# Two of four operand sums made by accumulating transfers in a Fourier-mixing kernel

## The chip, the core and the metric

The kernel runs on one core of a Trainium2 chip. The metric is the device time of one execution in microseconds. One execution of each kernel is recorded by the hardware profiler; its lines are shown below as "profile".

A core has TensorE (PE, matrix products, with its weight loads shown as PEld), VectorE (DVE), ScalarE (ACT), GpSimd (POOL) and SyncE (SP). In this kernel SP issues all transfers, in the order of its own instruction stream, and an instruction that waits holds back what stands behind it on its engine.

## The reference, cut to what matters

```python
xn = layernorm(x)                                  # x: 2048 x 512, float32
a = xn @ dft_hid_re.T ; b = xn @ dft_hid_im.T      # 512 x 512
s = dft_seq_re @ a - dft_seq_im @ b                # 2048 x 2048
h = relu(xn @ w1 + b1) ** 2                        # hidden size 1792
g = silu(h @ w2 + b2)
out = x + s * g
```

## The kernel before

The kernel reorders the Fourier part: it first multiplies the normalised x with the sequence matrices (called C, the cosines and sines, 2048 x 2048 each) and then with the hidden matrices (`wd`). Every product is made in three passes of reduced-precision float32: an operand is split into a high half and a low half (`split`: ScalarE writes the high half, VectorE subtracts it from the source to get the low one), and the passes are high x high, high x low and low x high.

The columns of C are cut into eight blocks of 256 (`c`), the rows of C in steps (`j`, eight for each block). Blocks 0 and 1 (`PLAIN = 2`) are done with plain products, while x is being loaded and normalised. Blocks 2 to 7, the C stage, use Winograd's form of Strassen's scheme: one step takes the four sub-blocks I11, I12, I21, I22 of C (each 128 partitions x 256 columns, I22 etc. being places in the raw tile `r`) and needs, beside three of them as they are, four sums T1 to T4. The seven products of the step accumulate in seven banks M[1] to M[7] over the eight steps of a block; at the block's end VectorE and ScalarE combine the banks into four results and split them for `stage2`, which multiplies with `wd` (lines 493 to 509).

For one step the preparation is `load_c` (a transfer of 512 KB into `r`, three buffers) and `moving` (line 167): the sums into `t` (two buffers), then the split of `r` into `g0` (three sub-blocks, 768 columns) and the split of `t` into `g1` (four sums, 1024 columns); `g0` and `g1` have two buffers each. The sums are made by VectorE, in `winograd_moving`:

```python
t[:, 0:2] = r[I12] - r[I11:I22+1]     # L162, one instruction of 512 columns
t[:, 2]   = r[I22] - t[:, 0]          # L164, 256 columns
t[:, 3]   = t[:, 2] - r[I21]          # L165, 256 columns
```

Two steps are prepared ahead of their products (`AHEAD = 2`, `prep` at line 465). In the C stage there is other work beside the steps: `stage2` of the block before at steps 2 and 3, and jobs that prepare the weights of the second part (`make_w1`, `make_w2`) and store them in DRAM. After the C stage come the hidden products (`hidden`, line 404) and the outer products (`outer`, line 439).

The order of the instructions on each engine is not the order of the source: the program is built with a scheduler that plays the program through with its own costs and places each instruction on its engine's stream when it would be ready (`schedule_with_timeline_sim=True`, line 573). The order is then fixed; a change of one instruction can move others.

The names in the lines of the profile: `m` are the banks M, `g` the split operands `g0` and `g1`, `r` the raw tile, `t` the tile of sums, `xc` the stationary operand, `yps` the banks of `stage2`, `pq` its operands, `w1raw` a raw tile of w1, `hps` and `ops` the hidden and outer products.

Of the kernel before, what the change touches and what calls it, by code (L numbers as in the profile page):

```python
# [10 lines left out]
ALU = mybir.AluOpType  # L11

P = 128
# [3 lines left out]
CW = 256  # L17
# [5 lines left out]
PLAIN = 2  # L23
# [6 lines left out]
I12, I11, I22, I21 = range(4)  # L30
# [13 lines left out]
def fnet_gated_kernel(ctx, tc, x, xt, ct, wd, w1, w2, b1, b2, out):  # L44
    nc = tc.nc
# [5 lines left out]
    def split(hi, lo, src):  # L51
        cut[0] = nc.scalar.activation(hi, src, AF.Copy)  # L52
        return nc.vector.tensor_tensor(lo, src, hi.bitcast(F32), op=ALU.subtract)  # L53
# [14 lines left out]
    def bank(name):  # L68
        return acc.tile([P, 512], F32, tag="bank", name=name)

    def t2k(name):
        return pool.tile([P, 512], F32, tag="t2k", bufs=4, name=name)

    def buf(tag, shape, name, dtype=F32, bufs=1):
        return pool.tile(shape, dtype, tag=tag, bufs=bufs, name=name)
# [53 lines left out]
    def sums(g):  # L129


        s = xn32[ND * g, "tile"].rearrange("p j h (b n) -> p j (h b) n", b=2)
        t = s1[g] = buf("t", [P, ND, CW], f"s1_{g}", bufs=2)
        nc.vector.tensor_tensor(t, s[:, :, 1], s[:, :, 3], op=ALU.add)
        nc.vector.tensor_tensor(s[:, :, 1], s[:, :, 1], s[:, :, 0], op=ALU.subtract)
        nc.vector.tensor_tensor(s[:, :, 0], t, s[:, :, 0], op=ALU.subtract)
        return nc.vector.tensor_tensor(s[:, :, 2], s[:, :, 2], s[:, :, 0], op=ALU.subtract)

    def split_sums(j):
# [6 lines left out]
    raw, part = {}, {}  # L146

    def load_c(c, j, hs=slice(0, 2)):
        if (c, j) not in raw:
            raw[c, j] = buf("r", [P, 4, CW], f"r{c}_{j}", bufs=3)  # L150
        q = slice(2 * hs.start, 2 * hs.stop)
        nc.sync.dma_start(raw[c, j][:, q], ct[c, j, :, q])

# [7 lines left out]
    def winograd_moving(t, r):  # L161
        nc.vector.tensor_tensor(t[:, 0:2], r[:, I12:I12 + 1].to_broadcast([P, 2, CW]), r[:, I11:I22 + 1],  # L162
                                op=ALU.subtract)
        nc.vector.tensor_tensor(t[:, 2], r[:, I22], t[:, 0], op=ALU.subtract)  # L164
        nc.vector.tensor_tensor(t[:, 3], t[:, 2], r[:, I21], op=ALU.subtract)  # L165

    def moving(key, r):

        g0 = buf("g0", [P, 2, 3, CW], f"g0_{key}", F32R, bufs=2)
        g1 = buf("g1", [P, 2, 4, CW], f"g1_{key}", F32R, bufs=2)  # L170
        t = buf("t", [P, 4, CW], f"t_{key}", bufs=2)
        winograd_moving(t, r)
        split(g0[:, HI], g0[:, LO], r[:, I11:I21 + 1])
        split(g1[:, HI], g1[:, LO], t)
        return g0, g1
# [17 lines left out]
    def pq(c, m, dh, src=None):  # L193
        t = PQ[c, m, dh] = buf(f"pq{m}{dh}", [P, 2, 512], f"pq{c}_{m}_{dh}", F32R)
        if src is not None:
            split(t[:, HI], t[:, LO], src)
        return t

    def stage2(c, t):
        ps = bank(f"yps{c}_{t}")  # L200
        n = 0
        for m in range(2):
            for k in range(ND):
                w = (k % 2) * CW + t * P
                for a_, b_ in PASSES:
                    nc.tensor.matmul(ps, PQ[c, m, k // 2][:, a_, w:w + P], WD[m, k][:, b_, :],  # L206
                                     start=n == 0, stop=n == 2 * ND * 3 - 1)
                    n += 1
        if t == 0:
            ysb[c] = buf("sx", [P, 2, D], f"ysb{c}")  # L210
        y = ysb[c][:, t]
        nc.scalar.activation(y, ps, AF.Copy)
        nc.sync.dma_start(Y[2 * c + t], y)

    def mm(ps, w, mv, first, last):

        for d in range(2):
            for a_, b_ in PASSES:
                nc.tensor.matmul(ps[:, d * CW:(d + 1) * CW], w[:, a_, d * P:(d + 1) * P], mv(b_),  # L219
                                 start=first and d == 0 and (a_, b_) == (HI, HI),  # L220
                                 stop=last and (a_, b_) == (LO, HI), skip_group_check=True)
# [10 lines left out]
    def xt_half(c, q):  # L232


        st = xt_stage(c, q)
        if q == 0:
            flat = rows.rearrange("a b -> (a b)")
            xT["rows"] = st[0]
            for m in range(2):
                for h in range(2):  # L240
                    n = m * S + c * TC + h * 256
                    nc.sync.dma_start(st[0][:, 2 * m + 1 - h], bcast(flat[n:n + 256], 256))
        r, t = st[-2:]
        mr = xT["rows"]
        nc.sync.dma_start(r, xt[c, q])
        for k in range(2):
            nc.vector.tensor_tensor(r[:, 2 * k:2 * k + 2], r[:, 2 * k:2 * k + 2], mr[:, 0:2], op=ALU.subtract)
            nc.vector.tensor_tensor(r[:, 2 * k:2 * k + 2], r[:, 2 * k:2 * k + 2], mr[:, 2:4], op=ALU.mult)  # L248
        winograd_moving(t, r)
        g = xT[c, q] = buf(f"xc{q}" if c % 2 == 0 else f"wd{q}", [P, 7, 2, 256], f"xT{c}_{q}", F32R)  # L250
        split(g[:, 0:3, HI], g[:, 0:3, LO], r[:, I11:I21 + 1])
        split(g[:, 3:7, HI], g[:, 3:7, LO], t)
# [33 lines left out]
    for n, (c, j) in enumerate(order):  # L286
# [28 lines left out]
        if c == 1:  # L315
            with tc.issue_after(xn_lo[NJ - 1].ins):
                if j < 2:
                    sums(j)
                split_sums(j)
                split_s1(j)  # L320
                if j == 3 or j == 5:
                    for k in range(ND):
                        wd_split(j // 2 - 1, k)
            if j == 5:
                for t in range(2):
                    stage2(0, t)
        if j == NJ - 1:
            for dh in range(2):
                for m in range(2):
                    t = pq(c, m, dh)  # L330
# [49 lines left out]
    def load_w1(p):  # L380
        if p < NP - 1:
            t = buf(f"xc{2 + (p + 2) % 6}", [P, 7, 2, 256], f"w1_{p}", F32R)
            nc.sync.dma_start(t.bitcast(F32), W1D[p])
            W1[p] = [t[:, n] for n in range(7)]
        else:
            a = buf("g0", [P, 3, 2, 256], f"w1a_{p}", F32R, bufs=2)
            b = buf("g1", [P, 4, 2, 256], f"w1b_{p}", F32R, bufs=2)
            nc.sync.dma_start(a.bitcast(F32), W1D[p][:, 0:3])
            nc.sync.dma_start(b.bitcast(F32), W1D[p][:, 3:7])
            W1[p] = [a[:, n] for n in range(3)] + [b[:, n] for n in range(4)]  # L390
# [74 lines left out]
    def prep():  # L465
        while loads and len(raw) < 3:
            load_c(*loads.pop(0))
        if todo:
            s = todo.pop(0)
            part[s] = moving(f"{s[0]}_{s[1]}", raw.pop(s))  # L470

    for j in range(AHEAD):
        prep()

    M = None
    for c, j in steps:
        if j == 0:
            M = {p: bank(f"m{p}_{c}") for p in ORDER}
        g = part.pop((c, j))
        for p in ORDER:  # L480
            a, (grp, b) = PRODUCTS[p]
            mm(M[p], XC[j][:, a], lambda b_: g[grp][:, b_, b], j == 0, j == NJ - 1)
        if c == PLAIN:
            if j == 4:
                nc.vector.transpose(stats_t, stats.rearrange("p m h j -> p (m h j)"))
                for q in range(4):
                    nc.sync.dma_start(rows[:, q * 32:(q + 1) * 32], stats_t[q * 32:(q + 1) * 32, :])
        if j in (2, 3):
            stage2(c - 1, j - 2)
        if (c, j) in jobs:  # L490
            make, arg = jobs[c, j]
            make(arg)
        if j == NJ - 1:
            u = t2k(f"m1_{c}")
            nc.scalar.activation(u, M[1], AF.Copy)
            c11 = t2k(f"c11_{c}")
            nc.vector.tensor_tensor(c11, M[2], u, op=ALU.add)
            nc.vector.tensor_tensor(u, M[6], u, op=ALU.add)
            u3 = t2k(f"u3_{c}")
            nc.vector.tensor_tensor(u3, M[7], u, op=ALU.add)  # L500
            nc.vector.tensor_tensor(u, M[5], u, op=ALU.add)
            c22 = t2k(f"c22_{c}")
            nc.vector.tensor_tensor(c22, M[5], u3, op=ALU.add)
            nc.vector.tensor_tensor(u, M[3], u, op=ALU.add)
            nc.vector.scalar_tensor_tensor(u3, M[4], -1.0, u3, op0=ALU.mult, op1=ALU.add)
            pq(c, 0, 0, c11)
            pq(c, 1, 1, c22)
            pq(c, 1, 0, u)
            pq(c, 0, 1, u3)
        prep()  # L510
        if c == NC - 1:

            if j in (2, 3):
                xt_half(0, j - 2)
            elif j > 3:
                load_w1(j - 4)
# [83 lines left out]
```

## Time and profile before

| | us |
|---|---|
| median of three runs | 732.89 (732.84 to 734.55) |
| the profiled execution, its own time | 733.41 |
| its span, from the first instruction to the last | 731.5 |
| PE busy | 721.0 |
| VectorE busy | 547.6 |
| ScalarE busy | 255.2 |
| GpSimd busy | 0.2 |

The span is what the lines of the profile divide up; the profiled execution's own time is 1.9 us longer, for what lies around it. In a line with a bar, the figures behind the first bar are the busy time of the group in us and the mean time of one instruction in ns, those behind the second the idle time of the engine just before it, with what ended it. The granted clock of TensorE is 0.996 of full speed over the span. One transfer queue carries nearly all bytes: 132.95 MB in 43280 packets, 51.5% of the time of the 16 transfer engines.

### The profile page before, as it was taken

The numbers are of one execution on the slowest core, as the hardware profiler recorded it, in microseconds if no ns is written. First come the engines' busy times: TensorE is split into PE (matmuls) and PEld (weight loads), VectorE is DVE, ScalarE is ACT, GpSimd is POOL, SyncE is SP. The second block draws the span as 40 slices with busy tenths as digits, with TensorE's granted clock in tenths as the row PEclk, the third lists the DMA queues.
The fourth block names the chain that finished last, engine by engine and source line by source line (L and its number), as shares of the span: only waits on it lengthen the run. The fifth ranks groups of instructions, "written<-read, shape, count | busy, mean of one in ns | idle before, by whom it ended". The sixth has DMA issues, their size and how long they took to land.

```text
span 731.5 us, 11771 instructions
## 1 busy us (share of the span) xinstructions
PE 721.0 (99%) x4687; PEld 654.1 (89%) x4687; DVE 547.6 (75%) x976; ACT 255.2 (35%) x386; POOL 0.2 (0%) x4
## 2 busy tenths in 40 slices
PE   7999999999999999999999999999999999999997
PEld 4888889999999999999999989898889889889996
DVE  7999728588698697896795946957696789568447
ACT  4437424453544543453443421213131213122112
POOL 0000000000000000000000000000000000000000
PEclk9999999999999999999999999999999999999999
DMA  8622622473663853833833997442663265428331
GB/s 301 231 88 86 211 77 87 148 298 117 234 255 91 288 188 111 307 137 127 289 135 149 360 425 288 151 167 86 231 207 139 95 226 184 143 73 288 116 116 59
DMA packets 43335, 133.70 MB, mean 183 GB/s; under 512 B 5008, under 2 KB 7312, under 8 KB 40592
## 3 DMA queue, kind: packets, MB, share of 16 engines
q1 hardware_dynamic: 43280, 132.95, 51.5%
q8 instruction: 37, 0.61, 0.3%
q14 instruction: 18, 0.15, 0.1%
HBM read 104.34 MB, written 28.59 MB: 182 GB/s over the span
## 4 chain that ended last, share of the span: by engine, by line
PE 94%; DMA 2%; DVE 2%; ACT 1%; issue 1%; SPq 0%; DVEq 0%; ACTq 0%
PE m L219 33%; PE ops L441 19%; PE hps L414 17%; PE pq L309 13%; PE yps L206 12%; DMA w<-w2d 1%; DMA out<-fin 1%; DMA r<-in_ct 1%; DVE fin L457 0%; DVE fin L456 0%; ACT hh L52 0%; ACT g L52 0%; ACT z L455 0%; DVE z L454 0%; ACT xc L52 0%
## 5 line engine op out<-in xcount | busy, mean ns | idle before, releaser
L219 PEld LDWEIGHTS m<-g,xc 128*128 128x128 f32 x2016 | 242.6, 189 | 2.1
L219 PE MATMUL m<-g,xc 128*128 128x256 f32 x2016 | 243.2, 281 | 0.0
L441 PE MATMUL ops<-w,hh 128*128 128x512 f32 (+1 forms) x714 | 161.7, 381 | 0.4 <-ACT hh L52 0.3
L441 PEld LDWEIGHTS ops<-w,hh 128*128 128x128 f32 x714 | 126.5, 188 | 26.3 <-ACT hh L52 0.8
L414 PEld LDWEIGHTS hps<-xT,w 128*128 128x128 f32 x1008 | 123.3, 190 | 2.3
L414 PE MATMUL hps<-xT,w 128*128 128x256 f32 x1008 | 124.3, 281 | 0.0
L52 ACT ACTIVATE g<-r 128x768 fp32r<-128x768 f32 (+2 forms) x65 | 57.2, 888 | 128.9 <-PE m L219 99.3
L53 DVE TENSOR_TENSOR g<-r,g 128x768 fp32r<-128x768 f32 (+2 forms) x65 | 65.1, 1008 | 44.4 <-ACT g L52 44.2
L309 PE MATMUL pq<-g,xc 128*128 128x512 f32 x384 | 92.2, 400 | 3.7 <-ACT xc L52 3.7
L206 PE MATMUL yps<-wd,pq 128*128 128x512 f32 x384 | 94.1, 395 | 0.0
L309 PEld LDWEIGHTS pq<-g,xc 128*128 128x128 f32 x384 | 72.9, 190 | 22.4 <-ACT xc L52 4.5
L206 PEld LDWEIGHTS yps<-wd,pq 128*128 128x128 f32 x384 | 70.3, 188 | 15.1
L52 ACT ACTIVATE hh<-h 128x512 fp32r<-128x512 f32 x56 | 34.1, 630 | 116.4 <-DVE h L431 116.4
L53 DVE TENSOR_TENSOR g<-t,g 128x1024 fp32r<-128x1024 f32 x48 | 58.2, 1222 | 3.5 <-ACT g L52 3.3
L422 DVE SCALAR_TENSOR_TENSOR h<-hps,b1s,ht 128x256 f32<-128x256 f32 x28 | 13.5, 481 | 57.1 <-ACT ht L419 57.1
L52 ACT ACTIVATE g<-t 128x1024 fp32r<-128x1024 f32 x48 | 50.0, 1051 | 2.6 <-PE pq L309 2.6
L53 DVE TENSOR_TENSOR hh<-h,hh 128x512 fp32r<-128x512 f32 x56 | 36.8, 688 | 4.5 <-ACT hh L52 2.8
L431 DVE SCALAR_TENSOR_TENSOR h<-h 128x512 f32<-128x512 f32 x56 | 36.6, 685 | 0.3
L419 ACT ACTIVATE ht<-hps 128x256 f32<-128x256 f32 x28 | 10.7, 382 | 68.0 <-PE hps L414 68.0
L162 DVE TENSOR_TENSOR t<-r 128x512 f32<-128x512 f32 x48 | 32.5, 686 | 1.1 <-DMA r<-in_ct 0.8
L52 ACT ACTIVATE xT<-stage 128x768 fp32r<-128x768 f32 (+1 forms) x16 | 15.3, 955 | 45.8 <-DVE stage L248 28.2
L164 DVE TENSOR_TENSOR t<-r,t 128x256 f32<-128x256 f32 x48 | 19.8, 420 | 0.6
(85 smaller groups left out, 479.9 us busy)
## 6 DMA issues: line engine op xcount, KB each, us to landing
r<-in_ct SPq DMA_DIRECT2D x63, 512.0 KB, 3.4
w<-w2d SPq DMA_DIRECT2D x28, 512.0 KB, 4.0
w<-w2d SPq DMA_DIRECT2D x14, 1024.0 KB, 4.8
w1d<-w1g SPq DMA_DIRECT2D x21, 512.0 KB, 4.2
w<-w1d SPq DMA_DIRECT2D x6, 1792.0 KB, 13.8
w2d<-w2g SPq DMA_DIRECT2D x14, 512.0 KB, 5.2
y<-ysb SPq DMA_DIRECT2D x16, 256.0 KB, 4.2
stage<-in_xt SPq DMA_DIRECT2D x8, 512.0 KB, 5.2
```

What stands on the lines that cost most here:

```text
L52: cut[0] = nc.scalar.activation(hi, src, AF.Copy)
L53: return nc.vector.tensor_tensor(lo, src, hi.bitcast(F32), op=ALU.subtract)
L162: nc.vector.tensor_tensor(t[:, 0:2], r[:, I12:I12 + 1].to_broadcast([P, 2, CW]), r[:, I11:I22 + 1], op=ALU.subtract)
L164: nc.vector.tensor_tensor(t[:, 2], r[:, I22], t[:, 0], op=ALU.subtract)
L206: nc.tensor.matmul(ps, PQ[c, m, k // 2][:, a_, w:w + P], WD[m, k][:, b_, :], start=n == 0, stop=n == 2 * ND * 3 - 1)
L219: nc.tensor.matmul(ps[:, d * CW:(d + 1) * CW], w[:, a_, d * P:(d + 1) * P], mv(b_), start=first and d == 0 and (a_, b_) == (HI, HI), stop= ...
L309: nc.tensor.matmul(accs[k], w, g[:, b_, 2 * h:2 * h + 2], start=j == 0 and h == 0 and (a_, b_) == (HI, HI), stop=j == NJ - 1 and h == 1 an ...
L414: nc.tensor.matmul(M[n], W1[p][a][:, a_, q * P:(q + 1) * P], xT[c, q][:, b, b_], start=i == q == 0 and (a_, b_) == (HI, HI), stop=q == 1 a ...
L419: nc.scalar.activation(u, M[1], AF.Copy)
L422: nc.vector.scalar_tensor_tensor(h0[:, 0:256], M[2], c0, u, op0=ALU.add, op1=ALU.add)
L431: nc.vector.scalar_tensor_tensor(r, r, 0.0, r, op0=ALU.max, op1=ALU.mult)
L441: ins = nc.tensor.matmul(ps, H[c, f][:, a_, t * P:(t + 1) * P], W2[c, f][:, b_, cols], start=f == 0 and (a_, b_) == (HI, HI), stop=f == NF ...
```

## The change

In the C stage the first two sums of a step are no longer made by VectorE. SP issues a transfer that writes the sub-block I12 from DRAM into both places of `t`, and GpSimd issues a transfer that adds I11 and I22 from DRAM to them (`accum_op=ALU.add`). So that this and the two sums that stay on VectorE are additions, signs are turned in `sums` (which makes the sums of the stationary operand) and in the combination of the banks. I12 is no longer loaded into `r`, whose transfer is 384 KB.

```diff
@@ sums
-        nc.vector.tensor_tensor(t, s[:, :, 1], s[:, :, 3], op=ALU.add)
-        nc.vector.tensor_tensor(s[:, :, 1], s[:, :, 1], s[:, :, 0], op=ALU.subtract)
-        nc.vector.tensor_tensor(s[:, :, 0], t, s[:, :, 0], op=ALU.subtract)
+        nc.vector.tensor_tensor(t, s[:, :, 3], s[:, :, 1], op=ALU.subtract)
+        nc.vector.tensor_tensor(s[:, :, 1], s[:, :, 0], s[:, :, 1], op=ALU.subtract)
+        nc.vector.tensor_tensor(s[:, :, 0], t, s[:, :, 0], op=ALU.add)
@@ load_c
+        if c >= PLAIN:
+            nc.sync.dma_start(raw[c, j][:, I11:], ct[c, j, :, I11:])
+            return
@@ moving
-    def moving(key, r):
+    def moving(c, j, r):
...
-        winograd_moving(t, r)
+        nc.sync.dma_start(t[:, 0:2], ct[c, j, :, I12:I12 + 1].to_broadcast([P, 2, CW]))
+        nc.gpsimd.dma_start(t[:, 0:2], ct[c, j, :, I11:I22 + 1], accum_op=ALU.add)
+        nc.vector.tensor_tensor(t[:, 2], t[:, 1], r[:, I11], op=ALU.add)
+        nc.vector.tensor_tensor(t[:, 3], t[:, 2], r[:, I21], op=ALU.add)
         split(g0[:, HI], g0[:, LO], r[:, I11:I21 + 1])
         split(g1[:, HI], g1[:, LO], t)
@@ the end of a block
-            nc.vector.tensor_tensor(u, M[6], u, op=ALU.add)
+            nc.vector.tensor_tensor(u, u, M[6], op=ALU.subtract)
...
-            nc.vector.tensor_tensor(c22, M[5], u3, op=ALU.add)
-            nc.vector.tensor_tensor(u, M[3], u, op=ALU.add)
-            nc.vector.scalar_tensor_tensor(u3, M[4], -1.0, u3, op0=ALU.mult, op1=ALU.add)
+            nc.vector.scalar_tensor_tensor(c22, M[5], -1.0, u3, op0=ALU.mult, op1=ALU.subtract)
+            nc.vector.tensor_tensor(u, M[3], u, op=ALU.subtract)
+            nc.vector.tensor_tensor(u3, M[4], u3, op=ALU.add)
```

`winograd_moving` stays for the operands of the hidden products (`xt_half`), which are made as before. In the new kernel's lines the first transfer is L178, the adding one L179, the two sums that stay L180 and L181, and the seven products L228.

More of the change, by code (lines that the diff above doesn't have):

```diff
@@ L165, in winograd_moving @@
         nc.vector.tensor_tensor(t[:, 3], t[:, 2], r[:, I21], op=ALU.subtract)
-    def moving(key, r):
+    def moving(c, j, r):
+        key = f"{c}_{j}"
         g0 = buf("g0", [P, 2, 3, CW], f"g0_{key}", F32R, bufs=2)
@@ L469, in prep @@
             s = todo.pop(0)
-            part[s] = moving(f"{s[0]}_{s[1]}", raw.pop(s))
+            part[s] = moving(*s, raw.pop(s))
     for j in range(AHEAD):
```

## The prediction

> **What bounds the kernel now.** I read the page's first part for the engines, then the chain of work that ended last for the stage that the change touches, then the busy time of the engines in stretches cut at that stage's own period. I write (c, j) for step j of block c of the DFT, c from 2 to 7.
>
> ```profile
> span 731.5 us, 11771 instructions
> PE 721.0 (99%) x4687; PEld 654.1 (89%) x4687; DVE 547.6 (75%) x976; ACT 255.2 (35%) x386; POOL 0.2 (0%) x4
> ...
> L219 PE MATMUL m<-g,xc 128*128 128x256 f32 x2016 | 243.2, 281 | 0.0
> ```
>
> PE is busy for all but 10.5 us. The 2016 products take 243.2 us, so 0.1206 us each in the pipeline, and a step of 42 takes 5.07 us.
>
> ```profile
> 189.32 5.58 PE yps L206 x24
> 194.90 29.92 PE m L219 x252
> ...
> 240.34 5.58 PE yps L206 x24
> ```
>
> The same piece comes back after 240.34 - 189.32 = 51.02 us: one block, eight steps and the 48 matmuls of stage2.
>
> ```profile
> core 0: us, PE busy (x) PEld busy (x) DVE busy (x) ACT busy (x) POOL busy (x), PEclk, DMA share, GB/s
> 189.32:240.34 51.02, 51.02 (x385) 48.84 (x385) 40.49 (x63) 23.02 (x32) 0.00 (x0) 1.00 0.56 202
> 240.34:291.37 51.03, 51.03 (x386) 48.85 (x385) 40.48 (x63) 23.03 (x32) 0.00 (x0) 1.00 0.58 202
> ```
>
> In these blocks PE is busy for the whole 51.02 us at full clock, and VectorE for 40.49 us. So work taken from VectorE has nothing to give here. The blocks can only keep their length or grow, and what decides is how early each moving operand is ready.
>
> **What the change removes.**
>
> ```profile
> L162 DVE TENSOR_TENSOR t<-r 128x512 f32<-128x512 f32 x48 | 32.5, 686 | 1.1 <-DMA r<-in_ct 0.8
> L164 DVE TENSOR_TENSOR t<-r,t 128x256 f32<-128x256 f32 x48 | 19.8, 420 | 0.6
> L165 DVE TENSOR_TENSOR t<-t,r 128x256 f32<-128x256 f32 x48 | 19.7, 419 | 0.4
> ...
> HBM read 104.34 MB, written 28.59 MB: 182 GB/s over the span
> ```
>
> The L162 sums of the C blocks go: 48 of them, 32.5 us of VectorE, 5.5 us per block. Beside a PE that is 100% busy they are worth 0 on the path. The other two sums stay, 420 ns each, as additions. The turned signs in `sums` and in the evacuation leave as many instructions of the same shapes (seven on VectorE per block, of which one is a scalar_tensor_tensor before and after): 0.
>
> **What it adds.** For each of the 48 steps SP issues a transfer that writes C12 twice into t (256 KB), then GpSimd waits for its landing and issues a transfer that adds C11 and C22 (256 KB) into the same bytes. Only after the second may VectorE make the two remaining sums. GpSimd's queue holds nothing else, so its wait delays only its own later additions. SP gets 48 issues more, and each waits for a t buffer; the raw loads behind them have three buffers and stay ahead. The raw loads shrink from 512 to 384 KB; in all 18.9 MB more come from HBM than 104.34 before, which a DMA share of 0.56 to 0.58 can carry.
>
> So the cost is latency, and it falls into a loop, because t has two buffers. The first transfer for step j must wait until t of step j-2 has been split by VectorE (L53, g<-t). Before, the sums took 1.5 us of VectorE between those points; now there stands a delay D, from the split that frees t to the moment the sum may start.
>
> The bounds of D come from the nearest rows, plain loads.
>
> ```profile
> L353 SPq DMA_DIRECT2D w1raw<-in_w x14: 327/328/504, 79.0 to 347.1; - x14
> ...
> DMA to landing us min/median/max: 2.6/3.4/4.7
> ...
> L152 SPq DMA_DIRECT2D r<-in_ct x65: 327/328/1053, 1.2 to 390.1; - x65
> ...
> DMA to landing us min/median/max: 3.1/3.4/8.9
> ```
>
> A plain load of 256 KB lands 2.6 to 4.7 us after its issue, one of 512 KB 3.1 to 8.9. For the first transfer I take 3.0, between the smallest and the median of its size. For the adding one there is no row. It can't be under 2.6. It has to read the old bytes too, as many as the 512 KB load, so at least the median 3.4 is likely; at the other end I put twice that, 6.8. I take 5.0, near the middle of 3.4 and 6.8, since the add can be written only after both reads and the issue is made by software on GpSimd. D is then 8.0, with ends of 2.6 + 3.4 = 6.0 and 3.4 + 6.8 = 10.2.
>
> [...]
>
> **The loop.** The built program gives VectorE's order. For spacing I take the starts in this stretch, which overlap a little and are shorter than the durations.
>
> ```profile
> 211.04 1.23 DVE L53 TENSOR_TENSOR g<-t,g 128x1024 fp32r<-128x1024 f32 x1
> ...
> 215.52 0.41 DVE L165 TENSOR_TENSOR t<-t,r 128x256 f32<-128x256 f32 x1
> 215.85 0.95 DVE L53 TENSOR_TENSOR g<-r,g 128x768 fp32r<-128x768 f32 x1
> 216.72 1.22 DVE L53 TENSOR_TENSOR g<-t,g 128x1024 fp32r<-128x1024 f32 x1
> 217.85 0.68 DVE L501 TENSOR_TENSOR m<-m,m 128x512 f32<-128x512 f32 x1
> 218.45 0.68 DVE L503 TENSOR_TENSOR c<-m,u 128x512 f32<-128x512 f32 x1
> ...
> L52 ACT ACTIVATE g<-t x48: 1040/1046/1062, 107.2 to 409.9; 128x1024 fp32r<-128x1024 f32 x48
> ```
>
> That is 0.33 us for 256 columns, 0.87 for 768, 1.13 for 1024 and 0.60 for 512 on VectorE, and 1.05 for ScalarE's half of the split of t.
>
> For blocks 3, 4 and 5 the new order puts the evacuation of the block before ahead of the first split of t. Let E be the end of the block's last product. M[2] is done 30 products earlier, at E - 3.6, and VectorE starts the evacuation there. Up to and with the split of t of (c, 0) stand eleven operations of 512 columns (6.6), one of 768 (0.87), four of 256 (1.3) and the split (1.13), 9.9 us; for the waits on the way (M[7], M[5], ScalarE's halves) I put 0.7. The split ends at E + 7.0. Two small sums and the split of (c, 1) follow, +1.8: E + 8.8. From there:
> - step 3's transfers, D, then two sums 0.67 and the split of (c, 2) 1.13, which stands behind step 3's sums: D + 1.8;
> - step 4: D, sums 0.67, ScalarE's half 1.05, VectorE's 1.13: D + 2.9 (the split of r beside it is hidden under ScalarE);
> - step 6: D, sums 0.67, then the splits of (c, 5), which stand behind these sums: 0.87 + 1.13: D + 2.7;
> - step 7: D, its first sum 0.33, then the split of r of (c, 6), 0.87: D + 1.2, and PE may go on with step 6;
> - steps 6 and 7 on PE: 10.1, and the block ends.
>
> The fixed part is 8.8 + 1.8 + 2.9 + 2.7 + 1.2 + 10.1 = 27.5, and about 1.0 for some ten semaphores between engines (my estimate, 0.1 each): 28.5. A block then takes 28.5 + 4D, and it grows from D = (51.0 - 28.5) / 4 = 5.6 on. At D = 8.0 it is 60.5 us, +9.5.
>
> The sum: blocks 4 and 5, 9.5 each; block 3 uses up first what the splits are ahead, some 3 us (above, the split of t of (4, 0) ends at 211.04 + 1.23 = 212.27, and PE, which ends the first two steps of block 4 at 194.90 + 29.92 = 224.82, first takes it up about 8.6 us before that, near 216.2), so 6.5. Block 2 has no block before it whose evacuation stands ahead, and its first operands are prepared during the plain stage: I put 1. In blocks 6 and 7 the order takes the split of (c, 0) ahead of the last evacuations and lets sums and splits alternate, which by the same spacings makes the fixed part 5 us shorter: 4.5 each. Together 9.5 x 2 + 6.5 + 1 + 4.5 x 2 = 35.5 us, all in the C stage; the hidden and outer products behind it keep their instructions. Against this execution's span of 731.5 (733.41 for its own time, 1.9 around the span, and 732.89 the median of the runs) that is 767.0 in the span and 768 as a median.
>
> There is a second cost of the order alone. Behind E, PE has 24 products of the next two steps that need only r, 2.9 us, before it wants the high half of t of (c, 0). By the same list VectorE ends the second sum of that t some 2.6 us before that split ends (two pq splits, a small sum, the split itself: 0.60 x 2 + 0.33 + 1.13), at E + 4.4, and ScalarE's half at E + 5.4: 2.5 us of waiting in each of blocks 3 to 5, 7.5 us, however fast the transfers are. At D = 8.0 it lies inside the loop and isn't counted again.
>
> **The rivals.**
> - **Not slower.** The transfers are covered: D stays under 5.6 us, and the scheduler's late split costs nothing since PE runs behind. For it: plain 256 KB loads land in 2.6 us at best, and two of those are 5.2. Against it: the second also reads its destination, and the order alone gives 7.5 us by the list. Its time is 731.5 in the span and 733 as a median; below that there is nothing to win, as PE has no idle time in the blocks. Chance 0.07, of which 0.02 for a gain over 0.3% (an idle stretch outside the blocks that moves).
> - **Order alone.** D of 6.0 or less, and the 7.5 us at the three block ends are what is left: 740 to 743. This and the forecast are one mechanism at two sizes of D; chance 0.13 for under 746. [...]
> - **Far slower.** The adding transfer is slow in the DMA engines or waits on GpSimd's software, D of 12 and over. By four D per block in all six blocks each us of D costs 24 us: 768 + 4 x 24 = 864. For it: a 512 KB load took 8.9 us once. Against it: the share of the queues is about 0.57, so the engines have room. Chance 0.12.
> - **The forecast**, D between 6.2 and 10.2: chance 0.68.
>
> **How the numbers follow.** The time is the forecast's, 768. The lower end is the order alone, 740 with the surroundings of the span: 741. The upper end is D = 10.2, 2.2 x 24 = 53 us over the forecast: 821. That leaves out the first rival and the third, 0.19. About 0.3%, 2.2 us, is what a measurement of this kernel can tell from no change. Faster 0.02, same 0.05, slower 0.93.
>
> **What would show it.** In the profile after: the POOL row with 48 transfers; landings of the adding transfers near 5 us; VectorE waiting for DMA at the first of the remaining sums, some 0 to 3 us at a time, mostly at steps 2, 4, 6 and 7; PE no longer at 100% in a block, with idle time before the m products that name ACT g and DVE g, at the block's first step and around its step 6; the stretch of a block near 60 us in the middle blocks; the hidden and outer products as long as before. I would be wrong in the size if the adding transfer lands in under 3.5 us or over 7, and wrong in the mechanism if the blocks stay at 51 us, or if PE waits for r instead of t, or if the time goes into the stages after the C stage.

## The result and the profile after

The kernel with the change takes 821.23 us (median of 4 runs, 819.89 to 825.53) against 732.90 us before (4 runs, 732.84 to 734.55): a ratio of 1.121, with a 95% interval of 1.116 to 1.126. The forecast was 768 us with a range of 741 to 821. The direction was right; the loss is 88 us and not 35, just outside the range. The profiled execution took 825.53 us, 823.7 of them in the span.

The page of the changed kernel, in the lines that answer to those of before:

```profile
span 823.7 us, 11968 instructions
PE 750.4 (91%) x4687; PEld 676.2 (82%) x4687; DVE 517.9 (63%) x928; ACT 256.0 (31%) x386; POOL 42.2 (5%) x52
...
PEclk9999999889989979979989988999999999999999
...
L228 PE MATMUL m<-g,xc 128*128 128x256 f32 x2016 | 269.0, 296 | 61.6 <-ACT g L52 33.8
...
L180 DVE TENSOR_TENSOR t<-t,r 128x256 f32<-128x256 f32 x48 | 20.3, 424 | 128.7 <-DMA t<-in_ct 128.7
```

VectorE is down by 30 us and now waits 128.7 us for the transfers into t, at the first of the two sums that it kept. PE waits 61.6 us before the m products, where it waited 0.0. And there is a second change in that row: the same 2016 products are busy for 269.0 us in place of 243.2. They are as many and as large; the row of the clock shows slices under 9 in the middle of the span, where the page of before has none.

The six blocks of the C stage, each from the end of the last product of the block before to its own (in each row the stretch, its length, the busy time and number of instructions of PE, PEld, VectorE, ScalarE and GpSimd, the granted clock, the DMA share, GB/s):

```profile
113.27:174.88 61.61, 53.95 (x387) 50.98 (x386) 29.74 (x47) 20.86 (x31) 7.85 (x9) 0.94 0.70 202
174.88:238.46 63.58, 56.62 (x387) 53.42 (x386) 35.51 (x57) 23.28 (x32) 6.98 (x8) 0.92 0.72 211
238.46:307.06 68.60, 56.38 (x387) 52.94 (x386) 35.43 (x57) 23.51 (x32) 6.99 (x8) 0.90 0.66 196
307.06:375.82 68.76, 55.96 (x387) 52.62 (x386) 34.74 (x58) 23.19 (x32) 6.11 (x7) 0.90 0.65 183
375.82:437.71 61.89, 53.70 (x386) 50.73 (x386) 36.42 (x59) 22.80 (x32) 6.99 (x8) 0.94 0.71 202
437.71:510.01 72.30, 58.53 (x389) 54.97 (x389) 42.43 (x64) 22.23 (x28) 6.11 (x7) 0.88 0.72 227
sum 396.74, PE 335.13 PEld 315.66 DVE 214.26 ACT 135.87 POOL 41.03; mean PE 55.85 PEld 52.61 DVE 35.71 ACT 22.65 POOL 6.84
```

Before, a block took 51.0 us and PE was busy for all of it; the six together took 306.4. Now they take 396.7, which is 90.3 more, nearly all of the 92.2 by which the span grew. The row splits that by itself: length less PE's busy time is idle time, 396.7 - 335.1 = 61.6 us; and PE's busy time has grown by 335.1 - 306.4 = 28.7 us for the same work.

One pass through the loop, from the timeline of block 4 (SP issues the first transfer for step 7, GpSimd the adding one, VectorE makes the sum, PE takes up step 6; the brackets give the idle time before and who ended it):

```profile
279.87 0.38 SPq L178 DMA_DIRECT2D t<-in_ct  x1
...
285.58 0.88 POOL L179 DMA_DIRECT2D t<-in_ct  x1 [11.39 <-DMA t<-in_ct]
...
290.13 0.58 PE L228 MATMUL m<-g,xc 128*128 128x256 f32 x1 [5.39 <-ACT g L52]
...
293.11 0.43 DVE L180 TENSOR_TENSOR t<-t,r 128x256 f32<-128x256 f32 x1 [3.03 <-DMA t<-in_ct]
294.46 15.61 PE L228 MATMUL m<-g,xc 128*128 128x256 f32 x107 [3.74 <-DVE g L53]
```

Here D is 293.11 - 279.87 = 13.2 us, and not 8.0. VectorE waits for the landing, its half of the split of r of step 6 stands behind that sum, and PE's last wait at step 6, 3.7 us, ends with VectorE's half of that split: the chain that the prediction wrote down. The wait of 5.4 us just before ends with ScalarE's half of the split of the same r, and that one stood behind splits of the second part's weights (`make_w2`), which waited for their load. The last row also shows the second effect: 107 products in 15.61 us are 0.146 us each, where they took 0.1206.

```profile
285.00:289.80 4.80, 0.00 (x0) 0.00 (x0) 1.11 (x2) 1.71 (x3) 0.88 (x1) 1.00 1.02 361
289.80:300.00 10.20, 6.13 (x27) 5.83 (x28) 6.25 (x9) 4.17 (x6) 0.07 (x1) 0.50 0.81 285
```

In the stretch in which PE idles the granted clock is 1.00; in the 10.2 us that follow, it is 0.50.

The loads of the weights also hold ScalarE up. Its waits for them over the whole execution:

```profile
ACT w2g L52 <- DMA w2raw<-in_w: 35.7, 9, 11.1
ACT w1g L52 <- DMA w1raw<-in_w: 21.0, 2, 13.8
```

Before, these waits were 9.9 and 5.7 us. In block 3 such a load, and not t, ends PE's waits at step 6 (3.6 and 0.8 us). The second transfer into t of step 7 had landed at 217.1, but the sum stands on VectorE behind splits of w2, which wait for ScalarE's halves, and these for the load:

```profile
221.23 0.63 ACT L52 ACTIVATE w2g<-w2raw 128x512 fp32r<-128x512 f32 x1 [9.39 <-DMA w2raw<-in_w]
...
223.66 0.69 DVE L53 TENSOR_TENSOR w2g<-w2raw,w2g 128x512 fp32r<-128x512 f32 x1 [1.08 <-ACT w2g L52]
224.27 0.42 DVE L180 TENSOR_TENSOR t<-t,r 128x256 f32<-128x256 f32 x1
```

### The profile page after: what moved, and what is told of

Same layout as the page of the kernel before. It is cut to its first block, busy times and chain, and to the rows that moved or that the text cites. A ratio compares the mean times of both kernels' runs of the same rounds, so it can differ in the third digit from the quotient of the medians.

```text
span 823.7 us, 11968 instructions
## 1 busy us (share of the span) xinstructions
PE 750.4 (91%) x4687; PEld 676.2 (82%) x4687; DVE 517.9 (63%) x928; ACT 256.0 (31%) x386; POOL 42.2 (5%) x52
## 3 DMA queue, kind: packets, MB, share of 16 engines
q0 software_dynamic: 6912, 12.59, 9.5%
## 4 chain that ended last, share of the span: by engine, by line
PE 50%; DMA 31%; DVE 10%; issue 5%; ACT 2%; SPq 0%; POOLq 0%; POOL 0%; DVEq 0%; ACTq 0%
DMA t<-in_ct 27%; PE ops L450 17%; PE hps L423 15%; PE pq L318 11%; PE m L228 5%; DVE g L53 4%; PE yps L215 3%; DVE t L180 2%; DMA w1raw<-in_w 2%; ACT g L52 1%; DMA stage<-in_xt 1%; DVE t L181 1%; DMA r<-in_ct 1%; DMA w2raw<-in_w 1%; DVE fin L466 0%
## 5 line engine op out<-in xcount | busy, mean ns | idle before, releaser
L228 PE MATMUL m<-g,xc 128*128 128x256 f32 x2016 | 269.0, 296 | 61.6 <-ACT g L52 33.8
L228 PEld LDWEIGHTS m<-g,xc 128*128 128x128 f32 x2016 | 262.3, 203 | 69.3 <-ACT g L52 35.9
L180 DVE TENSOR_TENSOR t<-t,r 128x256 f32<-128x256 f32 x48 | 20.3, 424 | 128.7 <-DMA t<-in_ct 128.7
L215 PEld LDWEIGHTS yps<-wd,pq 128*128 128x128 f32 x384 | 72.4, 193 | 15.9 <-ACT ysb L221 0.2
L53 DVE TENSOR_TENSOR g<-t,g 128x1024 fp32r<-128x1024 f32 x48 | 58.6, 1221 | 12.5 <-ACT g L52 10.9
L179 POOL DMA_DIRECT2D t<-in_ct x48 | 42.0, 880 | 443.7 <-DMA t<-in_ct 234.2
L431 DVE SCALAR_TENSOR_TENSOR h<-hps,b1s,ht 128x256 f32<-128x256 f32 x28 | 13.5, 481 | 56.5 <-ACT ht L428 56.5
```

Of the source, the lines that this page charges most:

```text
L179: nc.gpsimd.dma_start(t[:, 0:2], ct[c, j, :, I11:I22 + 1], accum_op=ALU.add)
L180: nc.vector.tensor_tensor(t[:, 2], t[:, 1], r[:, I11], op=ALU.add)
L431: nc.vector.scalar_tensor_tensor(h0[:, 0:256], M[2], c0, u, op0=ALU.add, op1=ALU.add)
```

## The experiments

All times are medians, taken beside runs of the kernel before, whose medians lay between 732.9 and 734.1 us.

### The signs alone

```diff
-        nc.sync.dma_start(t[:, 0:2], ct[c, j, :, I12:I12 + 1].to_broadcast([P, 2, CW]))
-        nc.gpsimd.dma_start(t[:, 0:2], ct[c, j, :, I11:I22 + 1], accum_op=ALU.add)
+        nc.vector.tensor_tensor(t[:, 0:2], r[:, I12:I12 + 1].to_broadcast([P, 2, CW]), r[:, I11:I22 + 1],
+                                op=ALU.add)
```

The raw loads are whole again.

> The sign turns alone: all four sums stay on VectorE, the first two as one addition, and the raw loads are whole. My theory (the loss is the delay D of the two transfers, run through the two t buffers, and the half clock behind PE's waits) has neither here: 733 us, within 2, PE 99% busy, no half clock in the C stage, no wait for DMA at t. Rival: the turned signs themselves cost something on VectorE or in the order at the block ends; then 740 (the 7.5 us of the order alone) or more.

733.93 us, ratio 1.0007 (0.9997 to 1.0017). The products are where they were:

```profile
L225 PE MATMUL m<-g,xc 128*128 128x256 f32 x2016 | 243.2, 281 | 0.0
```

The turned signs cost nothing, as the prediction had it.

### One transfer in place of two

```diff
-        nc.sync.dma_start(t[:, 0:2], ct[c, j, :, I12:I12 + 1].to_broadcast([P, 2, CW]))
-        nc.gpsimd.dma_start(t[:, 0:2], ct[c, j, :, I11:I22 + 1], accum_op=ALU.add)
+        nc.sync.dma_start(t[:, 0:2], ct[c, j, :, I11:I22 + 1])
```

> One transfer instead of two: a plain load of C11 and C22 from SP into t, C12 and its addition are left out. SP's 48 extra issues, the short raw loads and two sums on VectorE stay. My theory: D is that one landing, about 4.0 us as in the changed kernel, under the 5.6 us from which a block grows, so 731 to 741 (the upper end with the 7.5 us of the block ends). Rival, that the order of the block ends or the extra DMA issues cost the time whatever D is: 780 or more, with PE waiting as in the changed kernel.

734.37 us, ratio 1.0015 (1.0005 to 1.0025). The landings of that transfer, and the products:

```profile
L227 PE MATMUL m<-g,xc 128*128 128x256 f32 x2016 | 243.0, 282 | 0.0
```
```profile
L178 SPq DMA_DIRECT2D t<-in_ct x48: 327/328/1101, 77.6 to 400.1; - x48
...
DMA to landing us min/median/max: 2.5/3.2/6.5
```

With D at a median of 3.2 us, under the break-even of 5.6, the loop costs 1 us, at most 2, though VectorE has lost the same two sums to the DMA queues and SP has the same issues more. So neither SP's issues nor the work moved from VectorE cost the 88 us.

### The addition left out

```diff
-        nc.gpsimd.dma_start(t[:, 0:2], ct[c, j, :, I11:I22 + 1], accum_op=ALU.add)
+        nc.gpsimd.dma_start(t[:, 0:2], ct[c, j, :, I11:I22 + 1])
```

> The second transfer still comes from GpSimd, behind the first, into the same bytes, but as a plain copy: the addition is left out. Every instruction is at the same place as in the changed kernel. My theory takes the adding itself as dearer than a copy: the copy should land in 3.5 to 4.0 us in place of 5.1, D falls from 9.8 to between 8.2 and 8.7, and at 24 us per us of D the time is 783 to 795. Rival, that the price is GpSimd's issue by software and not the add: the copy lands in 5 us too, and the time stays at 815 to 826.

794.76 us, ratio 1.084 (1.081 to 1.087). GpSimd's transfers in this kernel, and then the answer to the same question for the changed one:

```profile
L179 POOL DMA_DIRECT2D t<-in_ct x48: 536/536/670, 82.5 to 458.9; - x48
...
DMA to landing us min/median/max: 2.9/3.3/8.1
```
```profile
L179 POOL DMA_DIRECT2D t<-in_ct x48: 865/871/1128, 83.8 to 485.3; - x48
...
DMA to landing us min/median/max: 3.7/4.7/11.8
```

A copy from GpSimd's queue lands in a median of 3.3 us, the adding one in 4.7, and GpSimd itself is busy 0.87 us in place of 0.54 to issue it. That queue, which is there only in the kernels in which GpSimd issues transfers, with the copies and then with the additions:

```profile
q0 software_dynamic: 3840, 12.59, 4.9%
```
```profile
q0 software_dynamic: 6912, 12.59, 9.5%
```

The same 12.59 MB take 9.5% of the time of the 16 engines' longer span in place of 4.9%. Over all 48 steps the mean D, from SP's issue to the second landing, falls from 9.8 to 8.6, and the time by 26.5 us: 23 us for each us of D, where the prediction had 24. That these agree so well is in part luck. The C stage of this kernel:

```profile
112.05:480.04 367.99, 327.97 (x2310) 310.50 (x2309) 214.16 (x335) 136.42 (x182) 25.27 (x47) 0.94 0.65 220
```

It is 28.8 us shorter than the changed kernel's 396.7, but 7.2 of that is PE's own busy time (335.1 there), which the slope did not have; the waiting fell by 21.6, about 19 us for each us of D. Of the loss of 88 us the addition itself makes 26.5; the other 61 stay with a plain second transfer.

### The addition twice

```diff
         nc.gpsimd.dma_start(t[:, 0:2], ct[c, j, :, I11:I22 + 1], accum_op=ALU.add)
+        nc.gpsimd.dma_start(t[:, 0:2], ct[c, j, :, I11:I22 + 1], accum_op=ALU.add)
```

> The adding transfer is made twice, the second behind the first (C11 and C22 are added twice). My theory: D grows by one landing and one issue, 5.1 + 0.65 us, to about 15.5, and four D per block in six blocks make 24 x 5.75 = 138 us more than the changed kernel, about 960, less where a wait now starts only later; half clock in the C stage well over the 68 us of the changed kernel. Rival, that the loss is bandwidth (bytes and not latency): 12.6 MB more on 205 GB/s is at most 60 us, 880 or less. Rival, that the loss is the order alone: 821 within 10.

928.86 us, ratio 1.267 (1.262 to 1.273), 107.6 us over the changed kernel. The row of the products:

```profile
L229 PE MATMUL m<-g,xc 128*128 128x256 f32 x2016 | 303.1, 313 | 133.1 <-ACT g L52 97.6
```

Both rivals, bytes (880 at most) and the order alone (821), fall. My number was too high: the mean D grew by 7.0 us to 16.8, more than I put, but each of these us cost 15 and not 24. The slope holds near the changed kernel, not far from it.

### Without the weights' traffic

```diff
-            nc.sync.dma_start(r[i], w1[p, :, 2 * i:2 * i + 2].rearrange("p b n -> p (b n)"))
+            if p == 0:
+                nc.sync.dma_start(r[i], w1[p, :, 2 * i:2 * i + 2].rearrange("p b n -> p (b n)"))
+            else:
+                r[i] = XC[i][:, 0].bitcast(F32).rearrange("p b n -> p (b n)")
...
-            nc.sync.dma_start(W1D[p][:, slot:slot + n], g.bitcast(F32))
+            if p == 0:
+                nc.sync.dma_start(W1D[p][:, slot:slot + n], g.bitcast(F32))
```

The same in `make_w2`; `load_w1` and `load_w2` read block 0.

> The change as it is, but the preparation of the weights keeps only its arithmetic: beyond the first w1 and w2 block its loads and stores are left out (it reads resident data, and the later stages load the first block's results each time). My theory: the long D of steps 7, 0 and 1 (10 to 16 us) comes from this traffic beside them, so there D falls to 8 to 9, its mean from 9.8 to about 8.5, and the time by 24 us per us to 780 to 795 (770 if the block ends gain from the order too). Rival, that D is long there for another reason (GpSimd, the way the adds queue behind each other, the y stores): D at steps 7, 0 and 1 stays over 10 and the time over 810.

783.7 us, ratio 1.068 (1.066 to 1.070). Step 7 of block 5 (the timeline above has that of block 4):

```profile
327.28 0.38 SPq L178 DMA_DIRECT2D t<-in_ct  x1
...
331.37 0.87 POOL L179 DMA_DIRECT2D t<-in_ct  x1 [2.05 <-DMA t<-in_ct]
```

The second transfer is issued 4.1 us after the first in place of 5.7, and lands in 4.0 us in place of 7.5. D at step 7 in blocks 2 to 7 was 12.8, 8.0, 13.2, 13.5, 12.3, 16.1 and is 13.7, 8.4, 8.3, 8.1, 8.0, 8.3. Block 2, where the first w1 and w2 blocks keep their transfers, is the one that stays long. At step 0 of blocks 3 to 7 it falls from 9.7 to 11.0 down to 8.5 to 9.2. So the traffic of the weights (stores of 512 KB and loads of 256 KB that SP issues in the same microseconds) made the D long that the prediction took as one value.

It was worth 38 us with all that hangs on it, and D is only a part of that. The mean D fell by 1.0 us, from 9.8 to 8.8. Block 3 has the same D at steps 3, 4, 6 and 7 in both kernels, 33.3 us in all, and yet is 7.4 us shorter than the 63.6 above:

```profile
176.22:232.45 56.23, 53.31 (x385) 50.46 (x384) 32.39 (x51) 21.79 (x30) 6.96 (x8) 0.97 0.58 140
```

The load of w2 that held this block's sum of step 7 is gone here. Over the C stage 11.3 of the 41.1 us gained are PE's busy time. How much the D, the waits for the weights' loads and the order of the work each make is not kept apart: with these transfers gone the scheduler also puts the sums and splits of (c+1, 0) ahead of the evacuation, as in blocks 6 and 7.

### The order of the block ends, with one fast transfer

The kernel with one transfer, with the sums and the split of t of (c, 0), c from 3 to 5, held back behind the evacuation:

```diff
-        nc.vector.tensor_tensor(t[:, 2], t[:, 1], r[:, I11], op=ALU.add)
-        nc.vector.tensor_tensor(t[:, 3], t[:, 2], r[:, I21], op=ALU.add)
+        def rest(after=None, last=None):
+            with tc.issue_after(after.ins) if after else ExitStack():
+                nc.vector.tensor_tensor(t[:, 2], t[:, 1], r[:, I11], op=ALU.add)
+                nc.vector.tensor_tensor(t[:, 3], t[:, 2], r[:, I21], op=ALU.add)
+            with tc.issue_after(last.ins) if last else ExitStack():
+                split(g1[:, HI], g1[:, LO], t)
...
             pq(c, 0, 1, u3)
+            if late:
+                late.pop()(mark[0], mark[1])
```

`mark[0]` is the evacuation's last sum, `mark[1]` its last split.

> One plain transfer in place of two (C12 and its addition left out), with the order of the changed kernel at the ends of blocks 2, 3 and 4: the evacuation stands on VectorE ahead of the sums and the split of t of (c+1, 0). My theory keeps the order's own cost of the prediction: PE waits about 2.5 us at the start of blocks 3 to 5, 7.5 us, and a window of 3.4 us at half clock behind each may add 1.7 us, so 740 to 746. Rival, that PE's lead hides the late split when the transfers are early: 734, as with one transfer and the scheduler's own order.

749.20 us, ratio 1.022 (1.020 to 1.023): 15 us over the same transfers in the scheduler's own order, and above the 740 to 746 that I expected. PE's waits, and the products:

```profile
PE m L236 <- ACT g L52: 8.1, 3, 2.7
```
```profile
L236 PE MATMUL m<-g,xc 128*128 128x256 f32 x2016 | 248.5, 285 | 9.2 <-ACT g L52 8.1
```

Three waits of 2.7 us, where the prediction had three of 2.5. The mechanism and its size hold. The time is twice that: with the small waits PE waits 9.2 us, and the products behind the waits are slower by 5.3 us, 14.5 of the 15 together. Around the second wait:

```profile
219.06:276.07 57.01, 53.95 (x386) 51.21 (x386) 36.19 (x56) 23.52 (x32) 0.00 (x0) 0.94 0.58 199
224.00:230.80 6.80, 5.56 (x21) 5.17 (x22) 5.12 (x9) 3.70 (x4) 0.00 (x0) 0.50 0.44 136
```

6.8 us at a clock of 0.50 behind (and just into the end of) one wait of 2.7 us.

### Waits of PE without any transfer

Is the half clock the doing of the waits, or of the transfers? In the kernel with the signs alone, PE is made to wait once in blocks 2 to 6:

```diff
+        if j == 5 and c in STALL:
+            sb = bank(f"stall{c}")
+            with tc.issue_after(done[0].ins):
+                first = nc.tensor.matmul(sb[:, 0:256], XC[7][:, 0, HI, 0:P], XC[7][:, 0, HI, :], start=True, stop=True)
+            nc.scalar.activation(sw, sb[:, 0:32], AF.Copy)
+            for k in range(STALL[c]):
+                nc.gpsimd.tensor_scalar_mul(sw, sw.bitcast(F32), 1.0)
+            with tc.issue_after(first.ins):
+                last = nc.tensor.matmul(sb[0:32, 256:512], sw, XC[7][:, 0, HI, :], start=True, stop=True)
...
```

> All four sums on VectorE (turned signs), no added transfers, so no wait of its own; instead PE is made to wait once ahead of step 5 of blocks 2 to 6: a matmul, a ScalarE copy of 32 columns, a chain of 2, 4, 8, 14 and 20 small GpSimd operations, and a matmul that reads the end of the chain; the products of the step stay behind it. These results are read by nobody. My theory: the half clock is what follows a wait of PE, whatever its cause: no window at half clock behind waits under 1.5 us, one of 3.4 us behind waits of 2 to 3 us, 6.8 or more behind 5 us and over, and a block costs 51.0 us, its wait, and half of its half-clock time. No trace shows the length of one such GpSimd operation; at 0.1 to 0.3 us each the waits sum to 8 to 20 us and the kernel to 742 to 765. Rival, that the half clock comes from the added transfers or the load: no half clock in the C stage, and blocks longer by the waits alone.

780.47 us, ratio 1.064 (1.062 to 1.066), above the 742 to 765 that I put: most of the GpSimd operations took 0.29 us, but the first of each chain 1.2 to 3.3, so the waits are longer. The five waits in PE's timeline, and the five blocks:

```profile
151.80 0.31 PE L497 MATMUL stall<-xc,sw 128*32 128x256 f32 x1 [3.24 <-POOL sw L495]
208.61 0.42 PE L497 MATMUL stall<-xc,sw 128*32 128x256 f32 x1 [4.15 <-POOL sw L495]
268.21 0.42 PE L497 MATMUL stall<-xc,sw 128*32 128x256 f32 x1 [6.17 <-POOL sw L495]
330.99 0.42 PE L497 MATMUL stall<-xc,sw 128*32 128x256 f32 x1 [10.05 <-POOL sw L495]
396.87 0.42 PE L497 MATMUL stall<-xc,sw 128*32 128x256 f32 x1 [12.24 <-POOL sw L495]
```
```profile
112.43:168.50 56.07, 52.83 (x389) 50.52 (x388) 36.33 (x57) 22.48 (x34) 1.77 (x2) 0.97 0.49 174
168.50:226.09 57.59, 53.44 (x389) 51.12 (x388) 40.76 (x64) 23.18 (x33) 2.68 (x4) 0.94 0.50 179
226.09:284.98 58.89, 52.72 (x388) 50.41 (x388) 40.69 (x64) 23.08 (x33) 4.07 (x8) 0.94 0.50 175
284.98:348.68 63.70, 53.65 (x389) 51.34 (x388) 41.55 (x68) 22.66 (x33) 7.24 (x14) 0.89 0.44 149
348.68:414.10 65.42, 53.18 (x389) 50.87 (x388) 41.56 (x68) 22.71 (x33) 8.92 (x20) 0.90 0.43 145
```

PE's busy time, 51.0 to 51.2 in such a block before, is 52.7 to 53.7: 1.6 to 2.6 us more in each block, some 0.7 of it the two added matmuls, for waits of 3.2 to 12.2. The 2016 products are busy for 252.1 us in place of 243.2, so 1.8 us more behind each of the five waits. No transfer was added here, so in this kernel the waits were enough to bring on the half clock. Its price over these five was one of each wait and hardly of its length. My rule, the wait and half of all the half-clock time, was too dear for the long waits: the trace has 6.8 us at half clock behind the second wait and 13.7 behind the fourth (a mean clock of 0.63 from 204.5 to 213.8 and of 0.57 from 320.9 to 336.7), but the fourth's begin 2.1 us after PE stopped, so 8 of them fall into the wait and cost nothing.

### Filling the wait

```diff
+        if j == 5 and c < NC - 1:
+            fill = bank(f"fill{c}")
+            with tc.issue_after(done[0].ins):
+                for k in range(FILLERS):
+                    nc.tensor.matmul(fill[:, 0:256], XC[7][:, 0, HI, 0:P], XC[7][:, 0, HI, :], start=True, stop=True)
```

> The change as it is, with 48 matmuls more on PE (128x256, 5.8 us at full clock, into a bank that nobody reads) between steps 5 and 6 of blocks 2 to 6, where PE otherwise waits. They give work and no use. My theory: the half clock follows PE's waits; with the wait filled, half clock in the C stage falls from 68 us to under 40, and the kernel gets no slower for the 240 matmuls (29 us of PE): 800 to 822. Rival, that the half clock has nothing to do with the waits (load or heat, say): 68 us of half clock or more, and 821 or more; if PE's own work set the pace, 821 + 29 = 850.

829.14 us, ratio 1.130 (1.126 to 1.134): 8 us slower than the changed kernel for 29.6 us more of PE's work, where I expected it to be no slower; and the C stage has 58 us at half clock, not under 40 (the mean clock over its span is 0.961, and 0.956 in the changed kernel). The time settles nothing, since the scheduler chose another order on VectorE with the new matmuls, and PE now waits at the block starts. But one kernel shows both places:

```profile
283.00:297.00 14.00, 14.00 (x120) 14.00 (x119) 8.72 (x15) 5.79 (x8) 0.00 (x0) 1.00 0.97 327
304.00:316.00 12.00, 8.31 (x44) 7.52 (x43) 8.86 (x14) 4.00 (x5) 1.16 (x2) 0.72 0.55 129
```

The first row is block 4 around the filled place: PE is busy throughout, the clock stays at 1.00, at a DMA share of 0.97. The second is the start of block 5, not filled: PE waits 3.7 of 12 us and the clock falls to a mean of 0.72. So load on the DMA engines alone does not halve the clock.

### A third buffer for t, and both cures together

```diff
-        t = buf("t", [P, 4, CW], f"t_{key}", bufs=2)
+        n = (c * NJ + j) % 3
+        t = buf("t" if n < 2 else "x3", [P, 4, CW], f"t_{key}", bufs=2 if n < 2 else 1)
```

The raw tile gives its third buffer for it in the C stage.

> The change as it is, with a third buffer for t (its place comes from the raw tile, which has two buffers in place of three in the C stage). Same transfers, same adds, same bytes. My theory: a first transfer then waits for the split of step j-3 and not j-2, so D = 9.8 has about a whole step of 5 to 6 us more to hide in; the loop lets go, PE has no wait over 1 us at m in the middle of a block, no or little half clock, 733 to 745 (the upper end if the raw tile with two buffers or the order of the block ends costs its 7.5 us). Rival, that bytes or DMA load set the pace, or GpSimd's issues: 790 or more, since none of these is changed.

765.8 us, ratio 1.043 (1.041 to 1.045): 55 us better with every transfer still made, but not the 733 to 745 that I expected.

```profile
L230 PE MATMUL m<-g,xc 128*128 128x256 f32 x2016 | 255.3, 287 | 17.9 <-ACT g L52 8.7
```

The loop through the buffers is most of the loss, and bytes or issues are not: D is even longer here (10.5 us in the mean). What of the rest? The raw tile, the long D, or VectorE's order. With one transfer and the raw tile at two buffers:

> One plain transfer in place of two (C12 and its addition left out), t with its two buffers, but the raw tile with two buffers in the C stage, as the kernel with the third t buffer has it. It tells whether the 33 us that the third t buffer left were the price of the raw tile. If two raw buffers cost nothing by themselves: 734, as with one transfer and three raw buffers; then VectorE's order and the long D are what is left. If they are the cause: 750 to 766, with VectorE or ScalarE waiting for r and PE behind them.

734.22 us, ratio 1.0012 (1.0001 to 1.0023): by itself the raw tile is not it. With the third buffer and without the weights' traffic:

> The third t buffer and the weights' preparation without its loads and stores together (the later stages load the first block's results). My theory: what the third buffer left, 33 us, came from D of 12 to 13 us at steps 0 to 2 beside the weights' traffic; with D at 8 to 9 there and a third buffer the loop is loose: 733 to 745, PE's waits at m under 6 us in all. Rival, that the rest is the raw tile with two buffers or the order of VectorE's work: 755 or more.

768.89 us, ratio 1.048 (1.045 to 1.051). My theory falls here: mean D fell by 1.2 us to 9.4, and the time did not follow. PE's waits and VectorE's line at the end of block 3 say what is late instead:

```profile
PE m L230 <- DVE u L519: 8.4, 4, 2.2
PE m L230 <- DVE g L53: 8.1, 5, 2.5
...
PE m L230 <- DVE c L516: 4.0, 4, 3.6
```
```profile
225.19 0.42 DVE L182 TENSOR_TENSOR t<-t,r 128x256 f32<-128x256 f32 x1 [5.10 <-DMA t<-in_ct]
...
228.00 0.68 DVE L516 TENSOR_TENSOR c<-m,m 128x512 f32<-128x512 f32 x1
```

The sum of the next block's t stands ahead of the evacuation in VectorE's queue, waits 5.1 us there for its transfer, and PE, which ended the block at 224.4, waits first for a split of r behind that sum, and then for the banks that the evacuation frees. With three buffers the wait moves from the loop to VectorE's order of work. That this makes the whole 33 us I only read from the trace; no kernel with another order there was tried.

## Why the prediction was right and wrong

- **VectorE's saving is worth 0**: right. One transfer takes the same 32.5 us from it and ends at 734.37.
- **Signs 0, SP's issues and the raw loads 0**: right, by the first two kernels. The stages behind the C stage kept their length, 313.7 us after the last block against 312.5.
- **The loop and its six legs**: right where D sets the pace. The chain of work that ended last runs in blocks 4 and 5 through the transfers of steps 3, 4, 6 and 7, as written, and the split of t of (4, 0) ends 7.0 us after the last product of block 3, as added up. PE waits at the block's first step, and at step 6, whose split of r stands behind the sum of step 7's t. The raw loads themselves have a small part: ScalarE's waits for them grew from 6.6 to 15.9 us, and the chain that ended last gives them 1% of the span and the transfers into t 27%. With the four legs' own D, 28.5 + their sum gives 65.9 us for block 4 (8.5, 7.9, 7.9, 13.2) and 65.9 for block 5 (8.6, 7.5, 7.8, 13.5); measured were 68.6 and 68.8, with a slow clock in both. Block 3 does not follow: 28.5 + 33.3 less its lead of 3 would be 58.8, and it took 63.6, since a load of w2 set its pace. That the splits of the weights stand in the same in-order streams is not in the sum. Nor did the prediction have a row for its 0.1 us for each semaphore; in block 4's chain most of these steps take 0.03 to 0.2 us.
- **The slope, 24 us per us of D**: near, and in part by luck. The kernel without the addition gives 23, of which some 19 are waiting; the one with two additions gives 15.
- **D = 8.0, the same for all legs**: this is the step that failed first. The mean was 9.8: a first landing of 4.0 us against 3.0, then 0.66 us until GpSimd issues the second transfer, which the prediction put at nothing, then a landing of 5.1 against 5.0. At the quiet steps the 8.0 was right: steps 2 to 6 of blocks 3 to 5 have 7.5 to 8.9, and the adding transfer landed in a median of 4.7. But step 7 had 12 to 16 in all blocks but one, and steps 0 and 1 had 9.7 to 12.5 from block 3 on, beside the weights' traffic. The trace of before had the weights' loads and stores at those steps. The prediction took the bandwidth as free because the mean share was 0.57, and that mean hides the bursts: in the 4.8 us before step 6 of block 4 resumes (above) the share is about 1, at 361 GB/s. That the adding transfer takes time for the old bytes as well was an estimate; what is measured is a median of 4.7 against 3.3 for the copy. No run shows the 6.2 at which the forecast's range of D begins: the smallest landing of the adding transfer was 3.7, and no leg of blocks 3 to 5 had a D under 7.5.
- **PE's clock**: missing from the sum. The prediction let PE run its products at 0.1206 us after any wait. PE's busy time in the C stage grew by 28.7 us. It was busy for 48.7 of the 68.3 us at half clock, so 24.4 us of the growth are the clock; the other 4.3 are about what 26 waits add, behind each of which the last product shows its whole 0.28 us and not the 0.12 of the stream. Taken off whole, that leaves 793 us, well inside the range; some of it would come back as waiting, since a PE that is early waits longer for the same transfer.
- **The blocks one by one**: the forecast had +1, 6.5, 9.5, 9.5, 4.5 and 4.5 for blocks 2 to 7; measured were +10.4, 12.6, 17.6, 17.7, 10.9 and 21.3. Block 2 has no evacuation ahead of it, but its step 7 has a D of 12.8 as the others do, and the loop was left out for it. Block 7 holds the longest D, 16.1.
- **The order alone, 7.5 us**: right as a wait (8.1), half of its price in time (15), mostly by the clock.
- **The rivals**: not slower and far slower by D of 12 in all legs are both out. The last one's place, a slow landing, is what happened at some of the legs.

So of the 53 us by which the forecast was short, up to 29 are PE running slower, and the rest, some 24 or more, is waiting: the uneven D, the weights' loads ahead of sums and splits, and the blocks that were counted too low. How these share it was not measured.

## What to carry to other kernels

A transfer put in place of a short engine operation inside a ring of two buffers puts its whole latency on each turn of the ring (here a mean D of 9.8 us for a sum of 0.69): count what is left of the turn, and compare with the landing time at the busiest step, not at the median. A neighbour's burst of transfers in the same microseconds made 12 to 16 us of 8 here. It also made late what those transfers feed, and held up the urgent work behind that in VectorE's fixed order: the sum of step 7 in block 3 began at 224.27, 7.2 us after its own transfer had landed. When a wait of PE is priced, add about 2 us for each one of some 2.5 us or more, for the clock that came back at half speed here (on the products alone 1.8 behind each wait, 8.9 us for five without transfers and 5.3 for three in the kernel with the late order). And another buffer helped only as far as VectorE's order of work let it, 821 us to 766: the wait moved to a sum that stands ahead of something urgent (5.1 us at the end of block 3 above).

## What the chip did that I had not expected

The granted clock of PE halved behind waits that are shorter than the stretch at half clock. In the changed kernel PE waits 2.44 us until 180.33, and the clock is at 0.51 from 180.6 to 184.1. In its C stage no shorter wait began such a stretch, and the longest wait without one is of 1.43 us. In the kernel with the late order 6.8 us at a clock of 0.50 go with one wait of 2.7 us, and the three such waits made the products 5.3 us longer. In the kernel with the made waits the one of 3.24 us is followed by 3.4 us at 0.50 (152.4 to 155.8), and the clock is 1.00 again from 156.0 on. From how long a wait on the clock halves is not shown more closely.

GpSimd is busy 0.87 us to issue an adding transfer of 256 KB, and 0.54 us for a copy of the same bytes; the one lands in a median of 4.7 us and the other in 3.3.
